# The last expert of a mixture of experts, taken a quarter of its hidden width at a time

## Chip, cores and metric

The kernel runs on one core of a Trainium2 chip. The metric is the device time of one execution in microseconds (us), median of several runs. The engines are named as in the profile: PE (matmul), DVE (vector), ACT (scalar), POOL (gpsimd) and SP, which here only issues DMA transfers.

## The reference

Three stages follow one another: attention with pooled queries, a first mixture of experts (MoE), and a second, soft one. Cut to the part that matters here:

```python
# first MoE: x is [2304, 512], 8 experts, F = 1024
for e in range(8):
    h = np.maximum(x @ w1[e], 0.0)          # [2304, 1024]
    out += P[:, e:e + 1] * (h @ w2[e])      # P: Sinkhorn-normalised gate
# second MoE on x = out: 8 experts with 4 slots each
logits = x @ phi                            # [2304, 32]
d = softmax over the 2304 rows of logits
slot_input = d.T @ x                        # [32, 512] -> 8 experts x 4 slots
slot_out[e] = np.maximum(slot_input[e] @ w1[e], 0) @ w2[e]
return softmax over the 32 slots of logits @ slot_out
```

## The kernel before

The first MoE works on nine blocks of 256 rows (`NBLK` = 9). A block's x lies in SBUF as a high and a low part (tiles `xs`, 1 MiB each); only three of them fit, so the blocks are kept in DRAM and `load_x(v)` fetches them again, three block visits ahead, into the tile that was read last. Each expert has four pieces of w1 (tiles `w`, one of them in `wp`; 1 MiB each with their low parts) for a quarter of F each. `g1(e, i, fp)` makes the quarter `fp` of h for block `i`: 24 matmuls of 256 columns, then a relu on ACT and the low part on DVE (tile `h`). Experts 0 to 6 go through `period`, which also runs the next block's `g1`. The last expert is written apart, in a loop over the blocks: four `g1` of the block, then `g2(e, i)`: for each half `t` of the block 24 matmuls of 512 columns (line 647 to 649) that sum over all of F in PSUM, then one DVE instruction that multiplies by `P` and adds to `acc[i]` (line 652). Its w2 lies in four pieces of tag `v`.

Into that loop the second MoE's first part is woven. `tail2_steps(i)` gives eight steps for block `i`: transposes of `acc` (`tr(0)`, `tr(1)`, tiles `tx` and `x2T`), `logit` (`l`), `fold` (`lf`, then a maximum on DVE and the exponential on ACT), `d_tok` (transposes `lt`, copied to `dT`), `slots` (`sl`), `soft` (`lt` again, then the softmax on DVE and ACT into `c`) and `ct`. They are put into the list `fill`; each call of `slot()` takes the next one. All engines but SP's DMA queue run in the order of the code. The steps take their PSUM from a pool `pm` of two banks.

The weights of the second MoE, 32 MiB, are fetched by `load_m2(tags)`, one letter per buffer: `v`, `w`, `p`, `x`, `0` are rooms of 1 MiB that the first MoE's tiles of that name leave, `a` and `o` rooms of half a MiB. First come 16 items of w1, then 16 of w2 (8 for each half `dh` of the output columns). SP issues all transfers in one queue, in the order of the code. After the loop `slot_input` follows, then for each half of the experts (`G`) the first product (line 1029), and for each `dh` the second (line 1059), a fold (line 1065), nine products with `ct` (line 1076), copies to `ot` (line 1080) and ten output transfers (line 1091).

Of the kernel before, what the change touches and what calls it, by code (L numbers as in the profile page):

```python
# [9 lines left out]
F32R = mybir.dt.float32r  # L10
# [349 lines left out]
def tile_attention__moe__softmoe(ctx, tc, q, k, v, w_gate, w1, w2, phi, m2_w1, m2_w2, out):  # L360
    nc = tc.nc
    N, D = out.shape
    E = w_gate.shape[1]
    FF = w1.shape[2]
    NBLK = N // 256
# [40 lines left out]
    pieces, staged = {}, {}  # L406
# [82 lines left out]
        nc.sync.dma_start(out=Xd[i], in_=X[i].rearrange("p z k n -> p (z k n)").bitcast(F32))  # L489

    def load_x(v):
        if NBLK <= v < E * NBLK:
            nc.sync.dma_start(out=x_tile(v).rearrange("p z k n -> p (z k n)").bitcast(F32), in_=Xd[v % NBLK])

    with ExitStack() as actx:
# [20 lines left out]
    def slot():  # L516
        if fill:
            f = fill.pop(0)
            if f is not None:
                f()  # L520
# [16 lines left out]
        nc.vector.tensor_tensor(out=o[:, 1], in0=src, in1=o[:, 0].bitcast(F32), op=ALU.subtract)  # L537


    def g1(e, i, fp):  # L540
        x = X[NBLK * e + i]
        ps = pg.tile([128, 512], F32, tag="g", name="g")
        w = pieces[e, fp].rearrange("p z (k f) -> p z k f", k=4)
        for f2 in range(2):
            o = ps[:, 256 * f2:256 * f2 + 256]
            c = slice(128 * f2, 128 * f2 + 128)
            for kk in range(4):
                nc.tensor.matmul(o, lhsT=w[:, 0, kk, c], rhs=x[:, 0, kk], start=kk == 0, stop=False)  # L548
                nc.tensor.matmul(o, lhsT=w[:, 0, kk, c], rhs=x[:, 1, kk], start=False, stop=False)  # L549
                nc.tensor.matmul(o, lhsT=w[:, 1, kk, c], rhs=x[:, 0, kk], start=False, stop=kk == 3)  # L550
        if fp == 0:
            Hh[i] = []
        if e == E - 1:
            Hh[i].append(m_p.tile([128, 2, 2, 256], F32R, tag="ho", name="h", bufs=4))
            h = Hh[i][-1].rearrange("p z f n -> p z (f n)")
            nc.scalar.activation(out=h[:, 0], in_=ps, func=AF.Relu)
            nc.vector.scalar_tensor_tensor(
                out=h[:, 1], in0=ps, scalar=0.0, in1=h[:, 0].bitcast(F32), op0=ALU.max, op1=ALU.subtract
            )
        else:  # L560
            if fp % 2 == 0:
                Hh[i].append(m_p.tile([128, 4, 256], F32, tag="hr", name="hr", bufs=2))
            h = Hh[i][-1][:, 2 * (fp % 2):2 * (fp % 2) + 2].rearrange("p f n -> p (f n)")
            nc.scalar.activation(out=h, in_=ps, func=AF.Relu)  # L564
        if fp == 3:
            load_x(NBLK * e + i + 3)

    written = set()
# [19 lines left out]
    def period(e, i, after):  # L588
        def then(name):
            for f in after.get(name, ()):  # L590
                f()

        def p(j):
            product(e, i, j)
            then(f"p{j}")

        def f(fp):
            g1(en, ni, fp)
            then(f"f{fp}")
            slot()  # L600

        en, ni = (e, i + 1) if i + 1 < NBLK else (e + 1, 0)
        if e == 0:
            acc[i] = xa_p.tile([128, 2, 512], F32, tag="xa", name=f"acc{i}")
        elif e == 1:
            for t in range(2):
                nc.vector.tensor_scalar(
                    out=acc[i][:, t], in0=acc[i][:, t], scalar1=P[:, 2 * i + t, 0:1], scalar2=None, op0=ALU.mult
                )
        for j in (2, 3, 4, 5):  # L610
            h_sum(i, j)
        h_split(i, 2)
        h_sum(i, 6)
        p(0)
        h_split(i, 3)
        p(1)
        slot()
        f(0)
        h_split(i, 4)
        p(2)  # L620
        slot()
        f(1)
        if en < E - 1:
            h_sum(ni, 0)
            h_sum(ni, 1)
        h_split(i, 5)
        p(3)
        h_split(i, 6)
        p(4)
        slot()  # L630
        if en < E - 1:
            h_split(ni, 0)
        f(2)
        p(5)
        if en < E - 1:
            h_split(ni, 1)
        p(6)
        slot()
        f(3)

    def g2(e, i):
        for t in range(2):
            ps = py.tile([128, 512], F32, tag="y", name="y")
            for f in range(8):
                h = Hh[i][f // 2][:, :, f % 2, 128 * t:128 * t + 128]
                w = pieces[e, 4 + f // 2].rearrange("p z (c d) -> p z c d", c=2)[:, :, f % 2]
                nc.tensor.matmul(ps, lhsT=h[:, 0], rhs=w[:, 0], start=f == 0, stop=False)  # L647
                nc.tensor.matmul(ps, lhsT=h[:, 0], rhs=w[:, 1], start=False, stop=False)
                nc.tensor.matmul(ps, lhsT=h[:, 1], rhs=w[:, 0], start=False, stop=f == 7)  # L649
                if f == 3:  # L650
                    slot()
            nc.vector.scalar_tensor_tensor(
                out=acc[i][:, t], in0=ps, scalar=P[:, 2 * i + t, e:e + 1], in1=acc[i][:, t],
                op0=ALU.mult, op1=ALU.add,
            )
            slot()
# [245 lines left out]
    def load_m2(tags):  # L902
        for tag in tags:
            pool, name, bufs = {
                "v": (m_p, "v", 7), "w": (m_p, "w", 4), "p": (wp_p, "wp", 1), "x": (m_p, "x", 2), "0": (wp_p, "x0", 1),
                "a": (xa_p, "xa", NBLK), "o": (m_p, "ho", 4),
            }[tag]
            if tag in "ao":
                kind, a, b = rest[0] if rest else queue.pop(0)
                n = 1 if kind == "w1" else 2  # L910
                lo = (2 * b if kind == "w1" else 0) + (n if rest else 0)
                rest[:] = [] if rest else [(kind, a, b)]
                t = pool.tile([128, 1024], F32, tag=name, name="m2h", bufs=bufs)
            else:
                kind, a, b = queue.pop(0)
                n, lo = (2, 2 * b) if kind == "w1" else (4, 0)
                t = pool.tile([128, 2048], F32, tag=name, name="m2w", bufs=bufs)
            load_part(t, kind, a, b, lo, n)
# [18 lines left out]
    def run(*fs):  # L937
        def f():
            for g, *a in fs:
                g(*a)  # L940
        return f
# [22 lines left out]
    for e in range(E - 1):  # L964
        n = e + 1
        for i in range(NBLK):
# [31 lines left out]
                if i + 2 < NBLK:  # L998
                    at("f0", (split_x, i + 2))
            period(e, i, after)  # L1000
    e = E - 1
    for i in range(NBLK):
        assert not fill
        before, now = (now if i else [None] * 8), tail2_steps(i)
        fill.extend(before[1:7] + now[:1] + before[7:])
        if i:
            for fp in range(4):
                g1(e, i, fp)
                slot()
        else:  # L1010
            for _ in range(4):
                slot()
        g2(e, i)
        load_m2({0: "vvvw", 4: "aa", 6: "0aa", 7: "x", 8: "xwwpwaa"}.get(i, ""))

    assert not fill
    load_m2("vvvvooooaa")
    for f in now[1:6]:
        f()
    slot_input()  # L1020
# [1 line left out]
    for G in range(2):  # L1022
# [11 lines left out]
        if G == 0:  # L1034
            for f in now[6:]:
                f()
        load_m2("vvvwaa0aax" if G == 0 else "xww")
        for half in range(2):
            nc.scalar.activation(out=hs[:, 512 * half:512 * half + 512], in_=ps[half], func=AF.Relu)
        for half in range(2):  # L1040
# [77 lines left out]
```

## Time and profile before

| | us |
|---|---|
| median of 3 runs (2272.35 to 2276.16) | 2273.21 |
| profiled execution: its own time | 2275.54 |
| profiled execution: span from first to last instruction | 2273.7 |
| PE busy in the span | 2191.6 (96%) |
| DVE busy | 1436.3 (63%) |
| ACT busy | 841.7 (37%) |
| last expert, from its first g2 to the end of its last (1976.5 to 2195.9) | 219.4 |
| from there to the end | 77.8 |

1.84 us of the profiled time lie outside the span. Times in the rows below are counted from the start of the span. A matmul's duration in a row reaches past the start of the next one, since they are pipelined; how far apart two of them start is what one costs.

### The profile page before, as it was taken

The page shows a single profiled execution, that of the slowest core. Times are in us where ns is not written, and L with a number is a line of the kernel's source. Part 1 is how long each engine was busy: PE and PEld are TensorE (multiplying, and loading weights), DVE is VectorE, ACT ScalarE, POOL GpSimd, SP SyncE. Part 2 cuts the span into 40 slices and gives each one's busy share as a digit, 9 for nine tenths or more (in the row PEclk, how much of TensorE's full clock was granted, in tenths as well). Part 3 has the DMA queues.
Part 4 walks back from the last instruction along what each step waited for, and adds up shares of the span by engine and source line. Part 5 has one row for each costly group of instructions (what it writes and reads, how often), then busy time and mean ns, then how long its engine had stood idle before and what let it go on. Part 6 is the DMA issues. An engine that isn't in the chain of part 4 may idle for free.

```text
span 2273.7 us, 40984 instructions
## 1 busy us (share of the span) xinstructions
PE 2191.6 (96%) x16789; PEld 1970.6 (87%) x16789; DVE 1436.3 (63%) x2660; ACT 841.7 (37%) x1779; POOL 583.8 (26%) x368
## 2 busy tenths in 40 slices
PE   7999999999899999999999999999999999999986
PEld 5666666666899999999999999999999999988863
DVE  5777777775667766685586568558656855622321
ACT  3555555555433432342243234224233422312211
POOL 5777777777100300030030003003001300100000
PEclk9999999999999999999999999999999999999997
DMA  7544544542211211122131122212112221411169
GB/s 178 129 105 108 136 115 99 135 107 72 84 48 75 102 57 66 58 92 71 42 103 56 66 69 82 75 38 103 57 66 80 71 75 38 154 51 56 63 229 310
DMA packets 121194, 211.39 MB, mean 93 GB/s; under 512 B 43696, under 2 KB 95408, under 8 KB 109744
## 3 DMA queue, kind: packets, MB, share of 16 engines
q1 hardware_dynamic: 121008, 208.77, 30.3%
q8 instruction: 133, 2.18, 0.4%
q14 instruction: 53, 0.43, 0.1%
HBM read 161.56 MB, written 14.16 MB: 77 GB/s over the span
## 4 chain that ended last, share of the span: by engine, by line
PE 74%; DVE 13%; issue 9%; ACT 1%; DMA 1%; POOL 1%; SPq 0%; ACTq 0%; DVEq 0%; POOLq 0%
PE g L548 10%; PE g L549 10%; PE g L550 10%; PE y L577 7%; PE y L576 7%; PE y L575 7%; PE o L234 6%; PE se L218 5%; PE S L189 4%; DVE rs L250 3%; DVE m L190 2%; DVE ho L537 2%; DVE ht L530 2%; PE y L647 2%; PE y L649 1%
## 5 line engine op out<-in xcount | busy, mean ns | idle before, releaser
L548 PE MATMUL g<-xs,w 128*128 128x256 f32 x2304 | 660.2, 287 | 0.0
L550 PE MATMUL g<-xs,w 128*128 128x256 f32 x2304 | 654.3, 284 | 1.1 <-DVE w L443 1.1
L549 PE MATMUL g<-xs,w 128*128 128x256 f32 x2304 | 654.5, 284 | 0.0
L575 PE MATMUL y<-v,ho 128*128 128x256 f32 x1764 | 503.6, 285 | 9.1 <-ACT ho L536 9.1
L577 PE MATMUL y<-v,ho 128*128 128x256 f32 x1764 | 503.6, 285 | 6.8 <-DVE ho L537 6.8
L576 PE MATMUL y<-v,ho 128*128 128x256 f32 x1764 | 502.4, 285 | 0.0
L548 PEld LDWEIGHTS g<-xs,w 128*128 128x128 f32 x2304 | 445.2, 193 | 7.7 <-issue 7.0
L550 PEld LDWEIGHTS g<-xs,w 128*128 128x128 f32 x2304 | 444.7, 193 | 1.3 <-DVE w L443 1.3
L549 PEld LDWEIGHTS g<-xs,w 128*128 128x128 f32 x2304 | 445.1, 193 | 0.3
L564 ACT ACTIVATE hr<-g 128x512 f32<-128x512 f32 x252 | 150.5, 597 | 773.8 <-PE g L550 757.7
L443 POOL TENSOR_TENSOR w<-stg,w 128x1024 fp32r<-128x1024 f32 x28 | 68.1, 2433 | 1194.6 <-ACT w L442 1194.6
L530 DVE TENSOR_TENSOR ht<-hr 128x512 f32<-128x512 f32 x315 | 230.1, 764 | 223.8 <-ACT hr L564 221.4
L575 PEld LDWEIGHTS y<-v,ho 128*128 128x128 f32 x1764 | 341.5, 194 | 10.4 <-ACT ho L536 10.4
L577 PEld LDWEIGHTS y<-v,ho 128*128 128x128 f32 x1764 | 342.0, 194 | 8.3 <-DVE ho L537 8.3
L576 PEld LDWEIGHTS y<-v,ho 128*128 128x128 f32 x1764 | 341.7, 194 | 0.0
L227 POOL TENSOR_TENSOR acc<-acc,e 128x576 f32<-128x576 f32 x224 | 318.7, 1423 | 73.8 <-ACT e L221 64.5
L585 DVE SCALAR_TENSOR_TENSOR acc<-y,P,acc 128x256 f32<-128x256 f32 x540 | 244.2, 477 | 118.0 <-PE y L577 118.0
L190 DVE TENSOR_REDUCE m<-S 128x1 f32<-128x384 f32 x432 | 234.0, 549 | 115.2 <-PE S L189 103.5
L221 ACT ACTIVATE e<-se 128x288 f32<-128x288 f32 x576 | 207.2, 411 | 153.6 <-PE se L218 134.5
L537 DVE TENSOR_TENSOR ho<-ht,ho 128x512 fp32r<-128x512 f32 x315 | 258.5, 820 | 7.0 <-ACT ho L536 6.9
L218 PE MATMUL se<-q,kd 128*128 128x288 f32 x1152 | 219.5, 309 | 7.6 <-ACT q L208 7.3
L536 ACT CAST ho<-ht 128x512 fp32r<-128x512 f32 x315 | 188.8, 618 | 81.0 <-DVE ht L530 78.6
(177 smaller groups left out, 2364.0 us busy)
## 6 DMA issues: line engine op xcount, KB each, us to landing
xs<-xd SPq DMA_DIRECT2D x63, 1024.0 KB, 4.8
stg<-in_moe_w_dram SPq DMA_DIRECT2D x60, 512.0 KB, 5.8
kd<-kp SPq DMA_DIRECT2D x32, 576.0 KB, 5.8
m2w<-in_moe_w_dram SPq DMA_DIRECT2D x13, 1024.0 KB, 9.4
m2w<-in_moe_w_dram SPq DMA_DIRECT2D x22, 512.0 KB, 8.6
kr<-in_k_dram SPq DMA_DIRECT2D x32, 288.0 KB, 6.8
qr<-in_q_dram SPq DMA_DIRECT2D x16, 576.0 KB, 4.0
kd<-kp SPq DMA_DIRECT2D x32, 288.0 KB, 3.6
```

Source lines behind the costliest of these rows:

```text
L190: nc.vector.tensor_reduce(out=M_[ph][:, x, n:n + 1], in_=ps, axis=AX.X, op=ALU.max)
L218: nc.tensor.matmul(ps, lhsT=kd[:, z, 128 * c:128 * c + 128], rhs=y[:, h, g], start=z == 0, stop=z == 1)
L227: nc.gpsimd.tensor_tensor(out=acc_[ph], in0=acc_[ph], in1=e, op=ALU.add)
L530: nc.vector.tensor_tensor(out=src, in0=q[0], in1=q[1], op=op)
L537: nc.vector.tensor_tensor(out=o[:, 1], in0=src, in1=o[:, 0].bitcast(F32), op=ALU.subtract)
L548: nc.tensor.matmul(o, lhsT=w[:, 0, kk, c], rhs=x[:, 0, kk], start=kk == 0, stop=False)
L549: nc.tensor.matmul(o, lhsT=w[:, 0, kk, c], rhs=x[:, 1, kk], start=False, stop=False)
L550: nc.tensor.matmul(o, lhsT=w[:, 1, kk, c], rhs=x[:, 0, kk], start=False, stop=kk == 3)
L575: nc.tensor.matmul(ps, lhsT=o[:, 0, c], rhs=v[:, 0, c], start=c == 0, stop=False)
L576: nc.tensor.matmul(ps, lhsT=o[:, 0, c], rhs=v[:, 1, c], start=False, stop=False)
L577: nc.tensor.matmul(ps, lhsT=o[:, 1, c], rhs=v[:, 0, c], start=False, stop=c == 3)
L585: nc.vector.scalar_tensor_tensor(out=y, in0=ps, scalar=p, in1=y, op0=ALU.mult, op1=ALU.add)
```

## The change

For the last expert the loops are turned round. The outer one is now the quarter `q` of F, the inner one the block: 36 visits `k = 9 q + i`. A visit calls `g1` for the visit three ahead and then `g2(k)`, which multiplies only the quarter's h (four tiles) with the quarter's piece of w2: 6 matmuls for each half of the block, then the DVE instruction that adds to `acc`. So each block is added to four times, and its x is loaded four times (`load_x` after each `g1` of this expert). The last `period` of expert 6 now makes quarter 0 of blocks 0 to 3, where it made four quarters of block 0. The steps of the second MoE stand in the last nine visits alone (`k` = 27 to 35): six slots a visit, two between `g1` and `g2` and four in `g2`, with `d_tok` and `soft` in one slot and `ct` and the next block's `tr(0)` in another. `g1` is not called in the last three visits. The lists of `load_m2` name the room of a quarter once it is done.

```diff
     def load_x(v):
-        if NBLK <= v < E * NBLK:
+        if NBLK <= v < (E + 3) * NBLK:
             nc.sync.dma_start(out=x_tile(v)...., in_=Xd[v % NBLK])
@@ g1
         if e == E - 1:
-            Hh[i].append(m_p.tile([128, 2, 2, 256], F32R, tag="ho", name="h", bufs=4))
-            h = Hh[i][-1].rearrange("p z f n -> p z (f n)")
+            Hh[i] = m_p.tile([128, 2, 2, 256], F32R, tag="ho", name="h", bufs=4)
+            h = Hh[i].rearrange("p z f n -> p z (f n)")
...
-        if fp == 3:
+        if fp == 3 or e == E - 1:
             load_x(NBLK * e + i + 3)
@@ period
         def f(fp):
-            g1(en, ni, fp)
+            if en < E - 1:
+                g1(en, ni, fp)
+            else:
+                g1(en, fp, 0)
@@
-    def g2(e, i):
+    def g2(k):
+        e, (q, i) = E - 1, divmod(k, NBLK)
+        w = pieces[e, 4 + q].rearrange("p z (c d) -> p z c d", c=2)
+        h = Hh.pop(k)
         for t in range(2):
             ps = py.tile([128, 512], F32, tag="y", name="y")
-            for f in range(8):
-                h = Hh[i][f // 2][:, :, f % 2, 128 * t:128 * t + 128]
-                w = pieces[e, 4 + f // 2].rearrange("p z (c d) -> p z c d", c=2)[:, :, f % 2]
-                nc.tensor.matmul(ps, lhsT=h[:, 0], rhs=w[:, 0], start=f == 0, stop=False)
-                nc.tensor.matmul(ps, lhsT=h[:, 0], rhs=w[:, 1], start=False, stop=False)
-                nc.tensor.matmul(ps, lhsT=h[:, 1], rhs=w[:, 0], start=False, stop=f == 7)
-                if f == 3:
+            for f in range(2):
+                c = slice(128 * t, 128 * t + 128)
+                nc.tensor.matmul(ps, lhsT=h[:, 0, f, c], rhs=w[:, 0, f], start=f == 0, stop=False)
+                nc.tensor.matmul(ps, lhsT=h[:, 0, f, c], rhs=w[:, 1, f], start=False, stop=False)
+                nc.tensor.matmul(ps, lhsT=h[:, 1, f, c], rhs=w[:, 0, f], start=False, stop=f == 1)
+                if f == 0:
                     slot()
             nc.vector.scalar_tensor_tensor(out=acc[i][:, t], in0=ps, ...)
             slot()
@@ the last expert's loop
-    for i in range(NBLK):
-        before, now = (now if i else [None] * 8), tail2_steps(i)
-        fill.extend(before[1:7] + now[:1] + before[7:])
-        if i:
-            for fp in range(4):
-                g1(e, i, fp)
-                slot()
-        else:
-            for _ in range(4):
-                slot()
-        g2(e, i)
-        load_m2({0: "vvvw", 4: "aa", 6: "0aa", 7: "x", 8: "xwwpwaa"}.get(i, ""))
-    load_m2("vvvvooooaa")
+    last = 3 * NBLK
+    for k in range(last + NBLK):
+        i = k - last
+        if i >= 0:
+            now = tail2_steps(i)
+            if i:
+                fill.extend([before[1], before[2], before[3], both(before[4], before[6]), before[5]])
+                fill.append(both(before[7], now[0]))
+            else:
+                fill.extend([None] * 5 + [now[0]])
+            before = now
+        if 3 < k + 3 < last + NBLK:
+            g1(E - 1, k + 3, (k + 3) // NBLK)
+        slot()
+        slot()
+        g2(k)
+        load_m2({0: "vvvw", 9: "vw", 18: "vw", 27: "vp", 31: "aa", 32: "0", 33: "aax", 34: "x", 35: "waa"}.get(k, ""))
+    load_m2("vooooaa")
@@ after the first product of G
-        load_m2("vvvwaa0aax" if G == 0 else "xww")
+        load_m2("vvvwvwvw" if G == 0 else "vpaa")
```

How the rows move on PE around a block's `logit`: before, a whole `g1` stands between the transposes `tx` and `l`, and another one behind `l`; its last rows ahead of `l` and its first behind it are

```order
L548 MATMUL g<-xs,w 128x256
L549 MATMUL g<-xs,w 128x256
L550 MATMUL g<-xs,w 128x256
L774 MATMUL l_22991<-x2T,ph 32x256 x4
L548 MATMUL g<-xs,w 128x256
L549 MATMUL g<-xs,w 128x256
```

and in the changed kernel (visit 30, block 2), right behind the last matmul of a `g1`:

```order
L769 MATMUL tx<-ident,acc_7335 128x128 x4
L780 MATMUL l_24174<-x2T,ph 32x256 x4
L653 MATMUL y<-v,h 128x512
L654 MATMUL y<-v,h 128x512
L655 MATMUL y<-v,h 128x512
L788 MATMUL lf<-misc,foldD 128x256
L653 MATMUL y<-v,h 128x512
L654 MATMUL y<-v,h 128x512
L655 MATMUL y<-v,h 128x512
L812 MATMUL lt<-ident,misc 128x128 x4
```

`l` reads what DVE copies out of `tx`, `lf` what ACT copies out of `l`, and `lt` what DVE and ACT make of `lf`: nothing stands between the first two now, three matmuls between the others. The four `lt` are two of `d_tok` and two of `soft`.

On DVE the same stretch held, before (`h` is the low part after a `g1`, `dnm` to `dsb` belong to `fold`, `dT` to `d_tok`, `misc` to `slots`):

```order
L557 SCALAR_TENSOR_TENSOR h<-g,h 128x512
L766 COPY x2T<-tx 128x4x128
L557 SCALAR_TENSOR_TENSOR h<-g,h 128x512 x2
L787 TENSOR_REDUCE dnm<-lf 128x1
L790 TENSOR_TENSOR dnm<-dnm 128x1
L791 TENSOR_TENSOR df<-dnm 128x1
L798 SCALAR_TENSOR_TENSOR dsb<-dsb,df 128x1
L557 SCALAR_TENSOR_TENSOR h<-g,h 128x512
L812 COPY dT<-lt 128x64
L844 SCALAR_TENSOR_TENSOR misc<-misc,df,sl 128x256
```

and holds now:

```order
L558 SCALAR_TENSOR_TENSOR h<-g,h 128x512
L772 COPY x2T<-tx 128x4x128
L793 TENSOR_REDUCE dnm<-lf 128x1
L796 TENSOR_TENSOR dnm<-dnm 128x1
L797 TENSOR_TENSOR df<-dnm 128x1
L804 SCALAR_TENSOR_TENSOR dsb<-dsb,df 128x1
L658 SCALAR_TENSOR_TENSOR acc_7607<-y,P,acc_7607 128x512
L818 COPY dT<-lt 128x64
L826 TENSOR_REDUCE cnm<-lt 128x2
L831 TENSOR_SCALAR csm<-csm 128x2
```

The copy `x2T` still stands behind the `h` of the `g1` before it; `dT` now stands behind an addition to `acc`, and the softmax of `soft` (from `cnm` on) right behind it.

On SP, from the room of quarter 2 to the first outputs (`m2w` and `m2h` are the second MoE's weights, line 888 or 894 w1 and line 896 or 902 w2; `xs` the blocks of x), before:

```order
L888 DMA m2w<-in_moe_w_dram 128x2x1024 x6
L888 DMA m2h<-in_moe_w_dram 128x1024 x2
L888 DMA m2w<-in_moe_w_dram 128x2x1024 x2
L896 DMA m2w<-in_moe_w_dram 128x4x256 x4
L896 DMA m2h<-in_moe_w_dram 128x2x256 x12
L896 DMA m2w<-in_moe_w_dram 128x4x256 x8
L896 DMA m2h<-in_moe_w_dram 128x2x256 x4
L896 DMA m2w<-in_moe_w_dram 128x4x256 x2
L896 DMA m2h<-in_moe_w_dram 128x2x256 x4
L896 DMA m2w<-in_moe_w_dram 128x4x256 x8
```

and now:

```order
L894 DMA m2w<-in_moe_w_dram 128x2x1024 x2
L493 DMA xs<-xd_8238 128x2048
L493 DMA xs<-xd_8514 128x2048
L894 DMA m2h<-in_moe_w_dram 128x1024 x2
L894 DMA m2w<-in_moe_w_dram 128x2x1024
L894 DMA m2h<-in_moe_w_dram 128x1024 x2
L894 DMA m2w<-in_moe_w_dram 128x2x1024 x3
L902 DMA m2h<-in_moe_w_dram 128x2x256 x4
L902 DMA m2w<-in_moe_w_dram 128x4x256 x2
L902 DMA m2h<-in_moe_w_dram 128x2x256 x12
L902 DMA m2w<-in_moe_w_dram 128x4x256 x20
L902 DMA m2h<-in_moe_w_dram 128x2x256 x4
```

Of w1's 16 MiB the loop now names ten by visit 27 and the rest by visit 35, with the first MiB of w2 at its end; before it named eight by block 7, six behind block 8, and two behind the loop.

## Rows read from the trace of the kernel before

**Rows 1.** Head of the profile page: the span, and PE's busy time, share and instructions.

```profile
span 2273.7 us, 40984 instructions
PE 2191.6 (96%) x16789; PEld 1970.6 (87%) x16789; DVE 1436.3 (63%) x2660; ACT 841.7 (37%) x1779; POOL 583.8 (26%) x368
```

**Rows 2.** Busy time by stretch: from:to, length, then busy time (and instructions) of PE, weight loads, DVE, ACT and POOL, the granted clock, the DMA engines' share and GB/s. One block of the last expert, the whole of it, what follows it, and the middle of that.

```profile
2046.60:2072.60 26.00, 26.00 (x180) 22.57 (x176) 7.72 (x19) 5.29 (x16) 0.00 (x0) 1.00 0.12 41
...
2195.90:2273.70 77.80, 51.06 (x473) 22.71 (x471) 14.32 (x40) 13.08 (x37) 0.00 (x0) 0.77 1.01 328
...
2206.00:2254.00 48.00, 38.64 (x409) 16.07 (x408) 6.59 (x22) 7.74 (x24) 0.00 (x0) 0.89 1.10 349
1976.50:2195.90 219.40, 219.40 (x1463) 189.97 (x1462) 62.32 (x151) 43.04 (x120) 0.00 (x0) 1.00 0.24 88
```

**Rows 3.** SP's own timeline: start, length, instruction, count. The last w1 loads and the outputs.

```profile
2157.41 28.65 SPq L888 DMA_DIRECT2D m2w<-in_moe_w_dram  x6
...
2248.36 22.40 SPq L1091 DMA_DIRECT2D out_dram<-ot  x20
```

**Rows 4.** PE's timeline behind the loop: the end of G = 0, the second product for dh = 0 (first row of it) with its fold, and the same for dh = 1. In brackets the idle time before the row and what ended it.

```profile
2211.80 3.61 PE L1029 MATMUL f<-m2w,misc 128*32 128x512 f32 x32
...
2228.49 1.93 PE L1059 MATMUL f<-m2w,HT 128*32 128x256 f32 x32
...
2236.15 0.70 PE L1065 MATMUL fd<-misc,foldD 128*128 128x256 f32 x2 [0.55 <-ACT misc L1063]
...
2240.62 1.07 PE L1059 MATMUL f<-m2w,HT 128*32 128x256 f32 x16
...
2255.50 1.08 PE L1059 MATMUL f<-m2w,HT 128*32 128x256 f32 x8 [0.24 <-DMA m2w<-in_moe_w_dram]
2257.12 1.22 PE L1065 MATMUL fd<-misc,foldD 128*128 128x256 f32 x2 [0.55 <-ACT misc L1063]
```

**Rows 5.** Timeline of the last stretch: the copies out of the last product, for dh = 0 (four on DVE, the first at the start given) and the first for dh = 1.

```profile
2239.05 2.48 DVE L1080 COPY ot<-op 128x512 f32<-128x512 f32 x4 [0.90 <-PE op L1076]
...
2261.04 0.69 DVE L1080 COPY ot<-op 128x512 f32<-128x512 f32 x1 [1.38 <-PE op L1076]
```

**Rows 6.** The chain that ended last, in the middle of the last expert: start, PE's time for the piece. One g1 matmul, `l`, a g2 matmul, the g2 matmul behind `sl`, and `tx`.

```profile
2046.45 0.57 PE l L774 x8
...
2049.72 0.12 PE g L548
...
2053.60 0.23 PE y L647
...
2056.91 0.43 PE y L647
...
2062.85 0.44 PE tx L763 x4
```

**Rows 7.** Timeline of PE and of DVE from 2038 to 2064: `tx` of one block behind a g1, and DVE's two instructions behind it.

```profile
2042.97 0.60 PE L763 MATMUL tx<-ident,acc 128*128 128x128 f32 x4
```

```profile
2043.86 0.69 DVE L557 SCALAR_TENSOR_TENSOR h<-g,h 128x512 fp32r<-128x512 f32 x1 [2.58 <-ACT h L556]
2044.47 0.68 DVE L766 COPY x2T<-tx 128x512 f32<-128x512 f32 x1
```

**Rows 8.** Timeline of all engines behind the loop: the same steps for the last block, where nothing stands between them.

```profile
2196.98 0.63 PE L763 MATMUL tx<-ident,acc 128*128 128x128 f32 x4 [0.72 <-DVE acc L652]
2197.64 0.69 DVE L766 COPY x2T<-tx 128x512 f32<-128x512 f32 x1 [0.35 <-PE tx L763]
...
2198.48 0.64 PE L774 MATMUL l<-x2T,ph 128*32 128x256 f32 x8 [0.87 <-DVE x2T L766]
...
2199.66 0.94 PE L782 MATMUL lf<-misc,foldD 128*128 128x256 f32 x2 [0.54 <-ACT misc L778]
...
2201.91 0.36 ACT L796 COPY misc<-lf 128x256 f32<-128x256 f32 x1
2201.97 0.69 PE L806 MATMUL lt<-ident,misc 128*128 128x128 f32 x2 [1.37 <-ACT misc L792]
2202.04 0.22 DVE L798 SCALAR_TENSOR_TENSOR dsb<-dsb,df 128x1 f32<-128x1 f32 x1 [0.59 <-ACT df L794]
...
2204.20 0.48 DVE L844 SCALAR_TENSOR_TENSOR misc<-misc,df,sl 128x256 f32<-128x256 f32 x1 [1.29 <-PE sl L839]
```

**Rows 9.** The same view a little later: the softmax of the last block, from its first DVE instruction to the transposes `ct`.

```profile
2215.81 0.22 DVE L820 TENSOR_REDUCE cnm<-lt 128x2 f32<-128x64 f32 x1 [9.14 <-PE lt L806]
...
2217.64 0.43 PE L853 MATMUL ct<-ident,c 128*128 128x128 f32 x2 [1.87 <-DVE c L828]
```

**Rows 10.** Groups of instructions from 1950 to the end: DVE's addition to `acc` in the last expert: busy time, mean ns.

```profile
L652 DVE SCALAR_TENSOR_TENSOR acc<-y,P,acc 128x512 f32<-128x512 f32 x18 | 13.5, 751 | 58.0 <-PE y L649 58.0
```

**Rows 11.** DMA issues of the page: a block of x, KB each, median us from issue to landing.

```profile
xs<-xd SPq DMA_DIRECT2D x63, 1024.0 KB, 4.8
```

**Rows 12.** Busy time by stretch, columns as in rows 2: four stretches in which PE waits much.

```profile
2196.00:2200.00 4.00, 1.87 (x17) 0.92 (x15) 1.87 (x3) 0.75 (x2) 0.00 (x0) 1.00 1.02 408
2200.00:2204.00 4.00, 2.22 (x12) 0.52 (x10) 1.19 (x5) 0.92 (x4) 0.00 (x0) 0.50 1.02 406
2216.00:2220.00 4.00, 1.40 (x10) 1.11 (x10) 1.28 (x7) 2.18 (x8) 0.00 (x0) 1.00 1.11 349
2244.00:2248.00 4.00, 1.67 (x24) 0.31 (x16) 0.00 (x0) 0.00 (x0) 0.00 (x0) 0.97 1.10 349
```

More of the change, by code (lines that the diff above doesn't have):

```diff
@@ L550, in g1 @@
                 nc.tensor.matmul(o, lhsT=w[:, 1, kk, c], rhs=x[:, 0, kk], start=False, stop=kk == 3)
-        if fp == 0:
+        if fp == 0 and e < E - 1:
             Hh[i] = []
         if e == E - 1:
-            Hh[i].append(m_p.tile([128, 2, 2, 256], F32R, tag="ho", name="h", bufs=4))
-            h = Hh[i][-1].rearrange("p z f n -> p z (f n)")
+            Hh[i] = m_p.tile([128, 2, 2, 256], F32R, tag="ho", name="h", bufs=4)
+            h = Hh[i].rearrange("p z f n -> p z (f n)")
             nc.scalar.activation(out=h[:, 0], in_=ps, func=AF.Relu)
@@ L1000, in tile_attention__moe__softmoe @@
             period(e, i, after)
-    e = E - 1
-    for i in range(NBLK):
+    both = lambda *fs: run(*[(f,) for f in fs])
+    last = 3 * NBLK
+    for k in range(last + NBLK):
+        i = k - last
         assert not fill
-        before, now = (now if i else [None] * 8), tail2_steps(i)
-        fill.extend(before[1:7] + now[:1] + before[7:])
-        if i:
-            for fp in range(4):
-                g1(e, i, fp)
-                slot()
-        else:
-            for _ in range(4):
-                slot()
-        g2(e, i)
-        load_m2({0: "vvvw", 4: "aa", 6: "0aa", 7: "x", 8: "xwwpwaa"}.get(i, ""))
+        if i >= 0:
[12 more added lines that the diff above has]
+        load_m2({0: "vvvw", 9: "vw", 18: "vw", 27: "vp", 31: "aa", 32: "0", 33: "aax", 34: "x", 35: "waa"}.get(k, ""))
     assert not fill
-    load_m2("vvvvooooaa")
+    load_m2("vooooaa")
     for f in now[1:6]:
```

## The prediction

> **What bounds the kernel now.** I read the page's head first, then the busy times by stretch. PE is busy 2191.6 of 2273.7 us [rows 1], and in the last expert 219.40 of 219.40: a block takes 26.00 us and PE never waits [rows 2]. DVE works 62.3 us there and ACT 43.0, so much of theirs is idle, and the DMA engines move 88 GB/s. Behind the loop it is the other way round: PE is busy 51.1 of 77.8 us while the DMA engines are full at 349 GB/s [rows 2]. The queue of SP shows why: six loads of w1 are issued between 2157.41 and 2186.06, most of what is left comes after, and the outputs of the first half start only at 2248.36, behind the last load [rows 3]. PE's timeline gives the price: the second product for dh = 0 goes from 2228.49 to 2235.60 (the fold at 2236.15 less 0.55 idle), 7.11 us; for dh = 1 from 2240.62 to 2256.58 (2255.50 and 1.08), 15.96 us, each step behind a DMA [rows 4]. So the loop is bound by PE, what follows it by DMA and by chains of short steps.
>
> **The matmuls stay the same.** 24 of `g1` at 0.12 and 12 of `g2` at 0.23 make a visit's 2.88 and 2.76 us [rows 6], 36 visits in both orders. Only their grouping changes. Up to visit 27 I see nothing to wait for: `h` is made three visits ahead, and DVE's share is one low part (0.69 [rows 7]) and two additions (0.75 each [rows 10]), 2.2 us in 5.6. The 54 more additions cost DVE 41 us, beside PE, with one exception below; without that cover they would cost their whole 41.
>
> **The 27 more loads of x.** A MiB takes 4.8 us from issue to landing [rows 11] and is asked for three visits later, of which about 14.0 us (three `g2`, two `g1`) are left once the tile is free. They raise the traffic by 28.3 MB over 219 us, 129 GB/s, to some 217, where 408 were moved in the stretch from 2196 [rows 12]. The tightest place is visit 4: its block is queued behind five MiB (one x, four of w1 from visit 0), 13 us at 408 GB/s, its own 2.6 and about 2.3 of latency (4.8 less the transfer's 2.5), so lands near 18 us after the loop starts; PE wants it at 4 x 2.76 + 3 x 2.88 = 19.7. Bounds: 0 and 3 us; I take 0. On SP, what would be stuck behind such a load is the next x, which has the same slack.
>
> **The eight steps are pressed into one visit.** Before, they lay spread over 26 us of a block, with a whole `g1` or several matmuls behind each. Now they share a visit of 2.88 + 2.76 us with their own work: 0.44 twice, `l` and `sl` 0.57, `lf` 0.43, three pairs of transposes at 0.22 (half of `tx`), and 0.2 each for the matmul behind `l` and `sl` (0.43 for 0.23) [rows 6]; together 9.15 us, 6.27 without `g1`. Each step waits for DVE or ACT, and PE takes its rows in order, so what is late stops all matmuls behind it. Counted from the end of `g1`:
>
> `tx` to `l`: DVE must first make `h` of the `g1` just done. `tx` started at 2042.97 and the copy behind it ended at 2045.15, 2.18 later [rows 7]; 0.15 more until `l` (from 2197.64 + 0.69 to 2198.48 [rows 8]): `l` at 2.33 where PE is free at 0.44. **1.9 us.** In the three visits without `g1` it is 2198.48 less 2196.98, 1.5, less 0.44: 1.1.
>
> `l` to `lf`: 1.18 from start to start [rows 8], and `l`, 0.2 and three matmuls last 1.46. Nothing.
>
> `lf` to `lt`: 1.37 idle behind `lf` [rows 8], which at full clock ends 0.6 after its start; 1.97 less 0.43 and three matmuls (0.69): **0.85.** The second `lt` wants ACT's copy, which ended at 2202.27, 0.30 after the first `lt` began [rows 8]; with 0.06 and less the 0.22 of the first: 0.14.
>
> `sl` wants `dT`, which DVE does after `dsb` (from 0.07 to 0.29 behind the start of `lt` [rows 8]) and now after an addition of 0.75 [rows 10]: 0.13.
>
> `ct` comes 1.83 after the start of `cnm` [rows 9], which stands behind `dT`; `sl`, 0.2 and six matmuls lie between: 0.24. The next `tr(0)` takes the bank that DVE frees with `misc` (0.48 [rows 8]) behind that softmax: 0.43.
>
> That is 3.7 us a visit with `g1`. Without it, `tr(1)` also waits until DVE has done the addition and the low part of `ct`, 0.7: 3.6. Visits 28 to 32 and 33 to 35: 5 x 3.7 + 3 x 3.6 = **29 us**. Below: the first two gaps alone, whose rows leave no doubt, are 5 x 2.7 + 3 x 1.9 = 19. Above: a further 0.2 us on each of some five hand-overs a visit, 37. I take 29, since every hand-over has its row.
>
> **What comes back behind the loop.** By the loop's end all of w1 and a MiB of w2 can be on the chip (the last rooms are free two visits ahead), and four more MiB of w2 need no product to finish; 4.2 MB at 349 GB/s are 12 us, done before G = 0 ends, 19.5 us after the loop (2215.41 less 2195.9 [rows 4]). The other 11 MiB wait for rooms of w1, as before; one of them frees early. Ten at 349 GB/s [rows 2] take 30.0 us: from 2215.4 with 2.3 of latency to 2247.7 in the old time. PE alone would end dh = 1 at 2240.62 + 7.11 = 2247.73. Both meet; with the last two groups behind the landing I take 2248.2, 8.4 us earlier than 2256.58. The clock then has no gap to fall in: from the end of the product to the first DVE copy for the output, 2261.73 less 2256.58 is 5.15 at the low clock, and 2239.74 less 2235.60 is 4.14 at the full one [rows 4, 5]: 1.0 more. From there to the end stay the 12.0 us of ten output issues. The ten of dh = 0 must be off SP by then; ten take about 9 us, from some 2242 to 2251, and the copy is due at 2252.3. Gain **9.4**; below, if the outputs or latencies take half of it, 5; above 10, since PE's 7.11 us remain.
>
> **Sum.** The profiled time is 2275.54, span 2273.7: 2273.7 + 29 - 9.4 = 2293.3 of span. The median of 2273.21 lies 2.3 under the profiled time; the difference put on it gives **2293**.
>
> **Rivals.** *The steps' latencies are hidden and only the gain shows:* DVE and ACT are idle two thirds of the loop, so their results could be there when PE comes. Then 2273 - 9.4 = 2264. It decides at 9.4 / 8 = 1.2 us a visit; the wait for `x2T` alone is 1.9 in five of eight [rows 7], which speaks against it. With stalls of 9 to 14 us it would be near no change.
>
> *The clock falls in visits 28 to 35.* PE was busy 1.87 of 4 us from 2196, and the clock was 0.50 in the next 4; it was 1.67 from 2244, and later rows go at half pace (the fold 1.22 for 0.70 [rows 4]); but 1.40 from 2216 left it at 1.00 [rows 12]. The new visits keep PE busy 9.15 of 12.8 us, and 6.27 of 9.9, with one gap of 1.9. At 1.2 GHz the work from `l` to `tr(0)`, near 5.5 us, doubles (`lf` 0.94 for 0.60 pipelined), of which the chains hide one: 4.5 a visit, 36 us, 2329. The Trainium skill's page "TensorE: Matmul & The Clock Gate", section "HAM oscillation — how this bites in real kernels", describes kernels whose clock drops at every group of matmuls because PE waits between them. By that rule, taken whole, the time would be this rival's 2329 and not 2293; the rows of these kinds of stretch are of both sorts, so I give it a tenth.
>
> *The gain doesn't come:* outputs or a late weight hold the end as before. 2273 + 29 = 2302.
>
> **Chances.** Forecast (2282 to 2305 by its bounds: 19 - 10 and 37 - 5) 0.70; hidden latencies 0.15, of it 0.09 faster, 0.05 within, 0.01 slower; clock 0.10; no gain 0.05. Two runs of this kernel can be told apart from about 0.2%, 4.5 us: faster 0.09, the same 0.05, slower 0.86. The range 2276 to 2308 takes in the third and half of the first rival's near cases, and leaves out the fast one and the full fall of the clock.
>
> **What would show it.** PE idle about 29 us between visit 28 and the loop's end and none before; the longest waits PE's `l` for DVE `x2T` (near 1.9) and `lt` for ACT `misc` (near 0.85); the granted clock 1.00 there; the second product for dh = 1 near 7.5 us with no DMA ahead of its rows; from the loop's end to the span's end about 68 instead of 77.8. Wrong if the visits 28 to 32 last under 10.5 us, if the clock falls in them, or if PE waits for `xs` before visit 27.

## The result, and the profile after

| | before | after |
|---|---|---|
| median of the runs compared, us | 2274.53 (2272.35 to 2276.16, 6 runs) | 2291.4 (2289.73 to 2295.43, 6 runs) |
| ratio to before, 95% interval | | 1.0076 [1.0063, 1.0089] |
| profiled execution: span, us | 2273.7 | 2288.0 |
| last expert, from the weight load of its first `g2` to the last start of a `g2` matmul | 219.0 | 242.8 |
| from there to the end | 78.1 | 70.5 |

The change costs 16.9 us; 19.6 were forecast (29 - 9.4). The 2291.4 lie in the range of the forecast 2293, and both parts came with their signs: a longer loop, a shorter rest. Both were taken too large, 29 for 23.8 and 9.4 for 7.6, and those errors partly cancel. That 2293 is only 1.6 off is partly luck: the kernel before also came out 1.3 us slower than the 2273.21 from which the forecast was counted. (In this profile the last expert begins 1.9 us earlier than before, in work that the change does not touch; in the profiles below this start varies from 1974.7 to 1978.7. So lengths are compared, not positions.)

The busy times by stretch, columns as in [rows 2]: the visits before 28, visits 28 to 35 (then, of these, the stretch of the five with `g1`, from behind their first `tx`, and the last three), and what follows the loop.

```profile
1974.70:2129.00 154.30, 154.30 (x986) 140.62 (x985) 60.71 (x84) 16.74 (x28) 0.00 (x0) 1.00 0.65 240
2129.90:2217.80 87.90, 70.00 (x468) 47.36 (x466) 40.65 (x121) 25.68 (x91) 0.00 (x0) 1.00 0.38 137
2133.20:2190.90 57.70, 45.88 (x313) 32.29 (x312) 26.82 (x77) 16.48 (x59) 0.00 (x0) 1.00 0.47 170
2190.90:2217.80 26.90, 20.82 (x127) 11.96 (x127) 13.43 (x44) 8.26 (x32) 0.00 (x0) 1.00 0.10 32
2217.80:2288.00 70.20, 45.67 (x477) 21.49 (x476) 14.39 (x42) 13.25 (x38) 0.00 (x0) 0.89 0.94 292
```

For the first 154 us PE is busy in all of them, as before, though DVE does the added additions and the DMA engines move 240 GB/s where [rows 2] had 88 over the loop. All the loss lies in the pressed visits, where PE is busy 70.00 of 87.90 us, at clock 1.00. (The 17.9 us without a busy PE are less than the loop's 23.8, since a row's duration reaches past the work of the row; the full loss is counted from start to start below.) What PE waited for in the last expert (engine, what, line; total us, times, longest):

```profile
PE l L780 <- DVE x2T L772: 11.0, 8, 1.7
PE lt L812 <- ACT misc L798: 5.1, 8, 0.7
PE tx L769 <- DVE ct L864: 0.9, 2, 0.5
PE tx L769 <- DVE miscr L864: 0.5, 1, 0.5
```

PE's timeline of one visit, from the `tx` behind its `g1` to the first `tx` of the next block:

```profile
2168.95 0.60 PE L769 MATMUL tx<-ident,acc 128*128 128x128 f32 x4
2171.21 0.64 PE L780 MATMUL l<-x2T,ph 128*32 128x256 f32 x8 [1.67 <-DVE x2T L772]
...
2172.58 0.59 PE L788 MATMUL lf<-misc,foldD 128*128 128x256 f32 x2
...
2174.55 0.79 PE L812 MATMUL lt<-ident,misc 128*128 128x128 f32 x4 [0.67 <-ACT misc L798]
...
2175.97 0.64 PE L845 MATMUL sl<-acc,dT 128*32 128x256 f32 x8
...
2177.37 0.43 PE L859 MATMUL ct<-ident,c 128*128 128x128 f32 x2
2177.87 0.66 PE L769 MATMUL tx<-ident,acc 128*128 128x128 f32 x4
...
2181.23 0.60 PE L769 MATMUL tx<-ident,acc 128*128 128x128 f32 x4
```

and DVE's in the same visit:

```profile
2169.77 0.69 DVE L558 SCALAR_TENSOR_TENSOR h<-g,h 128x512 fp32r<-128x512 f32 x1 [3.12 <-ACT h L557]
2170.38 0.68 DVE L772 COPY x2T<-tx 128x512 f32<-128x512 f32 x1
...
2174.62 0.22 DVE L804 SCALAR_TENSOR_TENSOR dsb<-dsb,df 128x1 f32<-128x1 f32 x1 [0.59 <-ACT df L800]
2174.75 0.74 DVE L658 SCALAR_TENSOR_TENSOR acc<-y,P,acc 128x512 f32<-128x512 f32 x1
2175.41 0.21 DVE L818 COPY dT<-lt 128x64 f32<-128x64 f32 x1
2175.55 0.21 DVE L826 TENSOR_REDUCE cnm<-lt 128x2 f32<-128x64 f32 x1
...
2177.33 0.48 DVE L850 SCALAR_TENSOR_TENSOR misc<-misc,df,sl 128x256 f32<-128x256 f32 x1
```

The copy `x2T` (2170.38 to 2171.06) stands behind `h`, and `l` starts 0.15 after its end: 2.26 us from `tx` to `l`, in which PE has 0.44 us to do.

Behind the loop, from PE's second product for dh = 1 to its first output product:

```profile
2262.46 5.82 PE L1070 MATMUL f<-m2w,HT 128*32 128x256 f32 x104
2268.57 0.64 PE L1070 MATMUL f<-m2w,HT 128*32 128x256 f32 x8 [0.29 <-DMA m2w<-in_moe_w_dram]
2269.32 0.63 PE L1070 MATMUL f<-m2h,HT 128*32 128x256 f32 x4
2270.71 1.27 PE L1070 MATMUL f<-m2h,HT 128*32 128x256 f32 x12 [0.77 <-DMA m2h<-in_moe_w_dram]
2272.51 0.70 PE L1076 MATMUL fd<-misc,foldD 128*128 128x256 f32 x2 [0.53 <-ACT misc L1074]
2274.68 1.66 PE L1087 MATMUL op<-miscr,ct 128*128 128x256 f32 x12 [1.47 <-DVE miscr L1080]
```

Eight of these matmuls took 1.08 us in [rows 4] and take 0.64 here, `fd` 0.70 instead of 1.22, and two short waits for a DMA are left. SP's queue around it, and the busy times by microsecond while it has nothing to send:

```profile
2219.02 8.52 SPq L902 DMA_DIRECT2D m2h<-in_moe_w_dram  x12
2233.82 27.44 SPq L902 DMA_DIRECT2D m2w<-in_moe_w_dram  x20
2261.35 3.48 SPq L902 DMA_DIRECT2D m2h<-in_moe_w_dram  x4
```

```profile
2232.00:2233.00 1.00, 1.00 (x12) 0.24 (x8) 0.00 (x0) 0.00 (x0) 0.00 (x0) 0.98 0.21 65
2233.00:2234.00 1.00, 1.00 (x12) 0.24 (x8) 0.00 (x0) 0.00 (x0) 0.00 (x0) 1.00 0.00 0
2234.00:2235.00 1.00, 1.00 (x16) 0.33 (x12) 0.00 (x0) 0.00 (x0) 0.00 (x0) 1.00 0.06 17
2235.00:2236.00 1.00, 1.00 (x16) 0.27 (x12) 0.00 (x0) 0.00 (x0) 0.00 (x0) 1.00 1.06 158
2236.00:2237.00 1.00, 1.00 (x12) 0.12 (x4) 0.00 (x0) 0.00 (x0) 0.00 (x0) 1.00 0.83 267
2237.00:2238.00 1.00, 0.60 (x6) 0.20 (x2) 0.22 (x1) 0.05 (x1) 0.00 (x0) 1.00 0.74 217
2238.00:2239.00 1.00, 0.00 (x0) 0.00 (x0) 0.33 (x2) 0.60 (x4) 0.00 (x0) 1.00 0.79 278
```

From 2232.2 to 2235 the DMA engines stand still: five MiB of w2 are on the chip by then, and the first room of w1 opens only halfway through the product of G = 0.

### The profile page after: what moved, and what is told of

Read it like the earlier page. It is cut to its first block, busy times and chain, and to the rows that moved or that the text cites. A ratio compares the mean times of both kernels' runs of the same rounds, so it can differ in the third digit from the quotient of the medians.

```text
span 2288.0 us, 41128 instructions
## 1 busy us (share of the span) xinstructions
PE 2189.1 (96%) x16789; PEld 1965.6 (86%) x16789; DVE 1475.6 (64%) x2714; ACT 840.5 (37%) x1779; POOL 583.5 (26%) x368
## 4 chain that ended last, share of the span: by engine, by line
PE 72%; DVE 14%; issue 9%; ACT 2%; DMA 1%; POOL 1%; SPq 0%; DVEq 0%; ACTq 0%; POOLq 0%
PE g L549 9%; PE g L550 9%; PE g L551 9%; PE y L578 7%; PE y L576 7%; PE y L577 7%; PE o L234 6%; PE se L218 5%; PE S L189 3%; DVE rs L250 3%; DVE m L190 2%; DVE ho L537 2%; DVE ht L530 2%; DVE v L468 1%; PE y L653 1%
## 5 line engine op out<-in xcount | busy, mean ns | idle before, releaser
L218 PE MATMUL se<-q,kd 128*128 128x288 f32 x1152 | 219.0, 309 | 7.7 <-ACT q L208 7.3
```

The costliest lines, as they stand in the source:

```text
L218: nc.tensor.matmul(ps, lhsT=kd[:, z, 128 * c:128 * c + 128], rhs=y[:, h, g], start=z == 0, stop=z == 1)
```

## Experiments

The theory: pressing the eight steps into one visit makes PE wait for the latency of DVE and ACT (the loop's +24), and the early weights shorten what follows the loop. Rivals: the quarters' own work costs (54 more additions, 27 more loads), or the clock. Lengths: "loop" from the weight load of the first `g2` to the last start of a `g2` matmul, "rest" from there to the end of the span, both of the one profiled execution; the changed kernel has 242.8 and 70.5.

**Quarters 0 and 1 through all blocks, then 2 and 3 together, block by block** (the last loop's visits have two `g1` and 24 `g2` matmuls for the six slots):

```diff
+    half = 2 * NBLK
+    for k in range(half):              # quarters 0 and 1, no steps
+        ...
+        g2(k % NBLK, k, (k // NBLK,))
+    for i in range(NBLK):              # quarters 2 and 3, steps as in the change
+        ...
+        for q in (2, 3):
+            if i + 1 < NBLK:
+                g1(E - 1, half + i + 1, q, q == 3)
+            slot()
+        g2(i, half + i, (2, 3))
```

> Quarters 0 and 1 go through all blocks as in the changed kernel, then quarters 2 and 3 together block by block, so a visit with the eight steps has 14.8 us of matmuls and a whole g1 or six matmuls stand between two steps; x is loaded three times instead of four. Theory (the loss is PE's waits between steps that stand too close): the gaps tx to l and sl to ct close, lf to lt keeps about 0.3 us; PE idle in the nine last visits falls from some 23 us to 3, the gain behind the loop (7 us) stays, since the same rooms for w1 are free by the loop's end: 2274.5 + 3 - 7 = 2270 (2267 to 2274). Rival (the visits themselves cost: the extra loads of x, the extra additions, the shorter sums in PSUM): of 27 more loads 18 remain and of 54 more additions 36, so two thirds of the 24 us remain: 2274.5 + 16 - 7 = 2283.

2272.75 us (11 runs), ratio to before 0.9991 [0.9982, 1.0000]; loop 223.2, rest 71.1. PE's waits up to the loop's end:

```profile
PE l L782 <- DVE x2T L774: 0.9, 1, 0.9
PE tx L771 <- DVE miscr L866: 0.6, 1, 0.6
```

Both stand in the last visit, which has no `g1`. With twice the matmuls between the steps the waits are gone, while 36 of the 54 further additions and 18 of the 27 further loads stay. The theory's 2270 was 2.8 us too low, the rival's 2283 is out. The rest is nearly that of the changed kernel, with a loop only 4.2 us longer than before: the early rooms give their gain without a long loop ahead.

**The kernel before with its steps pressed**, six slots a block as in the change, and nothing else:

```diff
-        fill.extend(before[1:7] + now[:1] + before[7:])
+        if i:
+            fill.extend([before[1], before[2], before[3], both(before[4], before[6]), before[5]])
+            fill.append(both(before[7], now[0]))
...
-                if f == 3:
+                if f < 2:
                     slot()
```

(with both first slots behind the four `g1`, and none behind the addition.)

> The kernel before, its order of quarters, loads and additions untouched, but the eight steps of a block pressed together as in the change: tx and l both behind the fourth g1, lf, the four lt, sl and ct with tx three matmuls apart inside g2 (18 matmuls follow lt and sl). Theory: per block 1.7 us idle ahead of l and 0.7 ahead of lt, 0.1 more for the second lt: 8 x 2.5 = 20 us, and nothing else changes: 2294 (2290 to 2298). Rival (the visits themselves cost, not the spacing): 2274.5, no change.

2292.24 us (4 runs), 1.0078 [1.0064, 1.0091]; loop 242.8, rest 72.9. Its waits in the loop:

```profile
PE l L773 <- DVE x2T L765: 13.7, 8, 1.7
PE lt L805 <- ACT misc L791: 4.7, 7, 0.9
```

So the pressing alone, with no quarter turned, costs the loop as much as the whole change, 23.8 us. That the two agree so closely is chance, since their waits differ (13.7 for `x2T` in eight visits with `g1` here, 11.0 there); that the turning itself is free is shown by the 154.30 busy of 154.30 us. The rest became 5.2 us shorter with no room named sooner, presumably since the loads had 24 us more. So a shorter rest alone doesn't prove the early rooms; the half-turned kernel above and the one without early weights below do.

**One transposition ahead of `g1`**, so that `h` and `x2T` are made beside it:

```diff
+        slot()
         if 3 < k + 3 < last + NBLK:
             g1(E - 1, k + 3, (k + 3) // NBLK)
         slot()
-        slot()
```

> The changed kernel with tr(1) moved ahead of g1, all else the same: g1's 2.9 us then lie between tx and l in visits 28 to 32. Theory: the idle time of l for x2T (1.67 us in each of these five) goes, while tx now waits about 0.5 us for the addition and the bank, as in visits 33 to 35: 5 x 1.2 = 6 us less, 2285.5 (2283 to 2287). Rival (the visits themselves cost): 2291, no change.

2290.06 us (4 runs), 1.0069 [1.0055, 1.0083]; loop 237.5, 5.3 us shorter; the waits in the loop are now

```profile
PE lt L812 <- ACT misc L798: 5.1, 8, 0.7
PE tx L769 <- DVE ct L864: 2.9, 6, 0.6
PE l L780 <- DVE x2T L772: 2.6, 3, 0.9
```

The wait for `x2T` goes in five visits, and 0.5 us for the bank of `tx` takes its place. But the rest was 73.4, and the median is only 1.3 us under the changed kernel's. Repeated:

> The kernel with tr(1) ahead of g1 once more: its loop was 5.3 us shorter than the changed kernel's and its time only 1.3, since the clock fell in more places behind the loop in the profiled execution (behind it 73.4 us where the changed kernel had 70.5). Theory (where the clock falls differs from execution to execution, not from code to code): loop 237.5 again, behind it 70 to 73.5, median 2287 to 2290. Rival (the code of this loop leaves the clock worse in each execution): 73.4 again and 2290.

2288.39 us (5 runs), 1.0060 [1.0046, 1.0073]; loop 237.4, rest 73.5. The median is 3.0 us under the changed kernel's and within the theory's 2287 to 2290, so how much of the 5.3 us arrives the runs leave open. The profile is the rival's: in both profiled executions the clock also fell behind the product of G = 0, here in the second and third of these rows, where the changed kernel kept 1.00:

```profile
2230.00:2234.00 4.00, 3.61 (x34) 0.92 (x26) 0.23 (x1) 0.03 (x1) 0.00 (x0) 1.00 0.72 168
2234.00:2238.00 4.00, 1.55 (x7) 1.38 (x8) 1.25 (x5) 1.98 (x7) 0.00 (x0) 0.72 1.07 349
2238.00:2242.00 4.00, 4.00 (x21) 1.25 (x23) 0.70 (x4) 0.69 (x4) 0.00 (x0) 0.50 1.10 353
2242.00:2246.00 4.00, 4.00 (x40) 1.16 (x36) 0.00 (x0) 0.00 (x0) 0.00 (x0) 0.92 1.10 347
```

Whether this loop always leaves it worse, and why, is open: these are two profiles.

**Without the further loads of x** (`X[v] = X[v - 3]` for quarters 1 to 3).

> Part left out: the 27 further loads of x for quarters 1 to 3 of the last expert; those quarters work on the three blocks that lie on the chip, so the output is not the reference's. Theory (the loads are hidden, PE never waits for xs): no change, 2291 us within 3, last loop 242.8. Rival (the loads cost something by traffic, or hold up the weights on SP's queue): faster by what they cost, over 5 us.

2291.52 us (4 runs), loop 242.8, rest 70.6. **Without the additions of quarters 0 to 2.**

> Part left out: the additions to acc after quarters 0, 1 and 2 (54 DVE instructions), so the output is not the reference's. Theory (they lie beside PE's work): no change, 2291 us within 3; last loop 242.8 because all 18 additions of quarter 3 are kept, ahead of the waiting steps. Rival (DVE's 41 us of additions are on the path): faster by over 5 and up to 41 us.

2291.53 us (4 runs), loop 242.8, rest 71.4. The loop by stretch: the changed kernel, without loads, and without additions:

```profile
1974.70:2217.50 242.80, 224.91 (x1456) 188.70 (x1455) 101.42 (x203) 42.43 (x119) 0.00 (x0) 1.00 0.55 204
```

```profile
1975.00:2217.70 242.70, 224.81 (x1456) 188.63 (x1455) 101.33 (x202) 42.42 (x119) 0.00 (x0) 1.00 0.24 87
```

```profile
1976.40:2219.10 242.70, 224.80 (x1455) 188.63 (x1455) 60.80 (x148) 42.43 (x119) 0.00 (x0) 1.00 0.54 204
```

With 87 GB/s instead of 204, or 60.8 us of DVE instead of 101.4, PE's time is the same to a tenth: both were rightly costed at nothing.

**The early weights undone**, the second MoE's loads after visit 18 put behind the loop:

```diff
-        load_m2({0: "vvvw", 9: "vw", 18: "vw", 27: "vp", 31: "aa", ..., 35: "waa"}.get(k, ""))
+        load_m2({0: "vvvw", 9: "vw", 18: "vw"}.get(k, ""))
-    load_m2("vooooaa")
+    load_m2("vvpaa0aaxxwaaooooaa")
```

> The changed kernel with only 8 MiB of the second MoE's weights named inside the loop; the next two loads name the room of quarter 2 and then that of quarter 3, which is free only when the loop ends, so 9 MiB instead of 17 are on the chip by then. Theory (the time behind the loop is set by what is still to be fetched there): 23 MiB follow the loop's end, 7 of w1 at 2.6 us and 16 of w2 at 3.0 us, 66 us, and 2 of latency, instead of 53 us until the last lands: 15 us more, 2306 (2302 to 2310), the loop unchanged. Rival (the gain behind the loop comes from the chains, not from the loads): 2291.

2309.09 us (4 runs), 1.0151 [1.0137, 1.0165]; loop 242.8, rest 88.9. So what the change names by visit 35 is worth 18 us to it, part of it perhaps by a lower clock (0.72 over the rest, 0.89 in the changed kernel); the loop does not notice those loads.

**w1 of the second MoE with the low and high halves sorted** (z first), meant to open four rooms halfway through G = 0 and so to close the DMA pause:

```diff
-    queue = [("w1", e, z) for e in range(E) for z in range(2)] + [
+    queue = [("w1", 4 * G + g, z) for G in range(2) for z in range(2) for g in range(4)] + [
```

> The changed kernel with w1 of the second MoE fetched z first inside each half of the experts, so that the first four rooms are free in the middle of the first half's product instead of one. Theory (the missing 1.8 us of the gain are the 4 us in which the DMA engines stand idle some 15 us behind the loop, for want of a room): last load some 1.5 to 2 us earlier, the product for dh = 1 near 7.5 to 8 us instead of 9.5, 2289.5. Rival (the last landing is set by something else: latency, the rate): 2291, dh = 1 still 9.5.

2292.08 us (5 runs), 1.0074 [1.0062, 1.0087]; loop 242.8, rest 72.0. The product for dh = 1 did take 7.4 us, with no DMA ahead of it, but it could do so for another reason: it began 48.5 us after the loop's last `g2`, not 44.9, and the clock over this rest was lower (0.82 for 0.89). This profiled execution was also the slowest of the five, 2295.24. Hence both kernels once more, side by side.

> The changed kernel once more, beside the next run: a second profile of the same code. Theory (the part up to the loop's end repeats, the clock behind the loop falls at places that differ between executions): last loop 242.8 again, behind it 70.5 to 72.5, 2291.5. Rival (the code sets where the clock falls): the same rows behind the loop as in the first profile, 70.5, no fall after the fourteenth us behind it.

> The kernel with z first once more, on the same chip as the changed one. Theory (the product for dh = 1 became 2.1 us shorter, 9.5 to 7.4, and a clock that fell elsewhere took it back in that one execution): the product 7.4 again, and the median 1 to 2 us below the changed kernel's of this comparison. Rival (the clock falls in each execution of this kernel, because PE does not wait for loads that late any more or for other reasons of its order): the same median within 0.5 us, the tail 72 again.

2292.15 us (4 runs) for the changed kernel and 2293.17 (4 runs) with z first; loop 242.8 both; rest 70.2 and 70.6. The product with z first:

```profile
2269.70 0.64 PE L1070 MATMUL f<-m2w,HT 128*32 128x256 f32 x8 [0.28 <-DMA m2w<-in_moe_w_dram]
2270.42 0.63 PE L1070 MATMUL f<-m2h,HT 128*32 128x256 f32 x4
2271.82 1.28 PE L1070 MATMUL f<-m2h,HT 128*32 128x256 f32 x12 [0.77 <-DMA m2h<-in_moe_w_dram]
```

The last twelve matmuls start 53.1 us after the loop's last `g2` (2271.82 less 2218.69), in the two profiles of the changed kernel 53.2 and 53.0. The theory of this edit fell: the 7.4 came from a PE that was late, not from an earlier load. SP's rows show why the edit could not help: it opened no room sooner. In the changed kernel five loads go out from 2233.8 to 2235.9, in the second profile of this one from 2235.0 to 2237.1, in both 16.3 to 18.4 us after the loop's last `g2`. So it was not want of rooms that slowed these first loads, and the expectation that the changed kernel has only one room there was wrong. In the first profile of z first the clock was the lower one, in the second it wasn't: where it falls can differ between executions of one kernel. The changed kernel's two profiles agree (0.89 and 0.90 over the rest), as the rival had it.

**The best kernel**: quarters 0 and 1 alone, 2 and 3 together, with `soft` moved from `d_tok`'s slot to that of `slots`, and `ct` of the last block put behind the loop; once with z first, once without.

```diff
-            fill.extend([before[1], before[2], before[3], both(before[4], before[6]), before[5]])
+            fill.extend([before[1], before[2], before[3], before[4], both(before[6], before[5])])
...
```

> Quarters 0 and 1 through all blocks, then quarters 2 and 3 together with the steps spread over 11.3 us of PE work a block, the softmax in the slot of slots and not of d_tok, ct of the last block behind the loop, and w1 of the second MoE z first. Theory (a step costs nothing once PE's work between two steps exceeds the engines' latency; the rest of the gain hangs on free rooms): loop 219 + 2 = 221, behind it 69 to 70, 2269 us, faster than both kernels. Rival (the clock behind the loop falls in other places and takes it back): 2273.

> The best kernel without z first: quarters 0 and 1 alone, 2 and 3 together, steps spread, w1 in the order of the experts as in the changed kernel. Theory (its gain over the first half-and-half kernel is the 1.2 us of stalls less in the loop, and z first gives nothing measurable because PE's own 7.1 us bound the last product there already): loop 222.0, 2271.2, as with z first. Rival (z first carried it): 2272.7.

2271.1 us (11 runs), 0.9983 [0.9974, 0.9991], with z first; 2271.08 (11 runs), 0.9984 [0.9975, 0.9993], without. Loop 222.0 in both, rest 71.9 and 73.6. Both are faster than the changed kernel, and faster than the kernel before by 0.16 to 0.17%; whether they are faster than the first half-and-half kernel (0.9991 [0.9982, 1.0000]) is not clear. z first gives nothing here either. The 69 to 70 us expected of the rest did not come: the clock was 0.84 and 0.81 over the rest, 0.89 in the changed kernel. (The 73.6 are from the slowest of the eleven executions, 2275.24.)

## Why the prediction was nearly right

**No wait before visit 28:** right, 154.30 of 154.30 us. PE never waits for `xs`, and the two runs that leave the loads or the additions out end at the same loop.

**The stalls, step by step.** From the visit above, starts less starts:

| from, to | measured | PE's own work | idle | forecast |
|---|---|---|---|---|
| `tx` to `l` | 2.26 | 0.44 | 1.82 | 1.9 |
| `l` to `lf` | 1.37 | 1.46 | -0.09 | 0 |
| `lf` to `lt` | 1.97 | 1.12 | 0.85 | 0.85 |
| `lt` to `sl` | 1.42 | 1.13 | 0.29 | 0.27 |
| `sl` to `ct` | 1.40 | 1.46 | -0.06 | 0.24 |
| `ct` to the next `tx` | 0.50 | 0.22 | 0.28 | 0.43 |
| `tx`, `g1` to `tx` | 3.36 | 3.32 | 0.04 | 0 |
| sum | 12.28 | 9.15 | 3.13 | 3.69 |

The three visits without `g1` last 9.3 and idle 3.05 by the same sum (1.13 from `tx` to `tx`, 1.53 on to `l`) for a forecast of 3.6. Eight visits make 24.8, the loop is 23.8 longer; 0.28 of the difference is the last `ct` to `tx`, which lies behind the loop's end, and some 0.6 is visit 28, the first of the eight, which takes 11.66 from `tx` (2132.65) to `tx` (2144.31). The mechanism held, and the two waits whose rows left no doubt were right to 0.1. The mis-sized term is the tail of small ones, the 0.24 for `ct` above all. `ct` does come 1.82 us after `cnm`, as [rows 9] had it; but `cnm` starts 1.00 after `lt`, some 0.27 earlier than counted, since I added whole durations of DVE's instructions, and these overlap: the addition starts 0.09 before `dsb`'s 0.22 is over, `dT` 0.08 before the addition's 0.74 is over, `cnm` 0.07 before `dT`'s 0.21. Starts less starts are what to add up, as for PE.

**The first rival** (latencies hidden) is out: 17.5 us of waits are listed, 11.0 of them for `x2T`. **The clock rival** is out: 1.00 throughout the pressed visits, with a gap of some 1.7 us in each of the five with `g1`, and PE busy 45.88 of 57.70. The rule of the Trainium skill that stood beside it ("TensorE: Matmul & The Clock Gate", "HAM oscillation — how this bites in real kernels") does not describe these visits. Behind the loop the granted clock did fall to 0.50 (1.2 GHz), after stretches in which PE was busy 1.40 and 2.05 of 4 us:

```profile
2220.00:2224.00 4.00, 1.40 (x11) 0.48 (x10) 1.43 (x4) 0.81 (x3) 0.00 (x0) 1.00 0.95 281
2224.00:2228.00 4.00, 2.05 (x12) 0.68 (x12) 1.51 (x6) 0.48 (x4) 0.00 (x0) 0.65 1.08 356
2228.00:2232.00 4.00, 3.65 (x20) 0.99 (x24) 0.49 (x2) 0.00 (x0) 0.00 (x0) 0.50 1.10 346
```

**The third rival** (no gain) is out by the 7.6 us.

**The gain behind the loop:** 7.6 of 9.4. The clock's 1.0 came: from the product's end (2271.98) to the first copy's end, 4.13 for a forecast of 4.14. The mis-sized step is "ten MiB at 349 GB/s, from G = 0's end". The last load was to land 51.8 us after the loop; the matmuls that wait for its last pieces start at 2270.71, 53.2 after the last `g2`'s start (52.8 after its end), and they are twelve, 1.27 us, so that the product ended 54.1 after the loop for 52.3. It took 9.5 us (from 2262.46), not near 7.5, and two waits for a DMA were left in it, where none was expected. The rooms opened 16.3 us behind that start, ahead of G = 0's end, and 11 MiB went out from there, not ten; these two errors nearly cancel: 33.0 us at 349 GB/s and 2.3 of latency would be 51.6, where 53.2 were measured. The rows from 2235 to 2239 show most of the remainder: 158, 267, 217 and 278 GB/s, 476 short of 4 x 349, or 1.4 us. After the standstill the rate takes four microseconds to come back, though SP had issued five loads, 2.5 MiB, by 2235.9; I had charged the latency alone. That this ramp is the cause is read from the rows, not shown by a run: the one edit aimed at the standstill opened no room sooner and left the landing where it was.

## What to carry to other kernels

Steps woven into a bound engine cost little as long as its own work between two of them exceeds the round trip through the other engines (here 2.3 us from a transposition through DVE, with one other instruction ahead there, to the next product); spread over 11 us of work a block they cost the loop 4.2 and 3.0 us in all, pressed into 5.6 they cost 3.1 a visit. So ask of an order that finishes inputs earlier how much cover it leaves the fine steps: half of the turning gave nearly all of the early rooms, 71.1 us of rest instead of 70.5, with few of the stalls. And a stretch after the change can become shorter just because the one ahead of it became longer, as in the pressed kernel before; that isn't the change's merit.

## What was not expected of the hardware

The clock behind the loop. Kernels with the same code from the last expert's end on had rests of 70.2 (clock 0.90 over the rest) to 73.5 us (0.80), by where the granted clock fell; the order with `tx` first lost 3 us there in both of its profiles, and z first 72.0 in one and 70.6 in the other. A gain of 2 us ahead of such a stretch may not arrive at the end. The overlap of successive DVE instructions (0.07 to 0.09 us each) was the other: the next starts before the row of the last one ends.
